# V weights ahead of x tiles 8 and 9 in the load order of a fused attention and gated block

## The chip, the cores and the metric

One core of a Trainium2 chip. The metric is the device time of one launch in microseconds; the granted TensorE clock was 1.000 in every profile, and every timed run counts as in the fast state (single looks are of unknown state by rule). "Look" below means one profiled execution. The span of a profile runs from its first to its last instruction and is some 1.3 us shorter than the device time.

## The reference

x is 2048 tokens of 640. Normalised, it goes through a windowed, dilated attention (32 heads of 20, window 8, dilation 2) with its output weights, and beside it through a gated product block; x and the two results are summed.

```python
xn = _layernorm(A_x)
# A: qkv = xn @ wqkv; each token attends to itself and 7 tokens at distances 2, 4 .. 14; @ wo
# B: (x @ w_gate) * (x @ w_up) @ w_down
return x + A(xn, wqkv, wo) + B(xn, w_gate, w_up, w_down)      # B_x is not used
```

## The kernel before

The kernel is tuned so that TensorE is busy nearly always. SyncE issues the loads of the first part in one list; the order of that list is all that the change touches.

```python
    for half, eng in ((0, "sp"), (1, "act")):     # x tile 0 in two halves
        ...
    x_load(1)
    for c in range(NCH):
        wqkv_load(0, c)          # Q weights, five pieces of 160 KB
    x_load(2)
    x_load(3)
    for c in range(NCH):
        wqkv_load(1, c)          # K weights, five pieces of 160 KB
    for t in range(4, 8):
        x_load(t)                # 160 KB each
    x_load2(8)                   # x tiles 8 and 9, 320 KB
    wqkv_load(2)                 # V weights, 800 KB in one transfer
    x_load2(10)
    x_load(12)
```

TensorE's program in that stretch: the Q weights on tiles 0 and 1 with 128 columns a matmul (source line L492, with the transposes of tile 1, L434, between), K on tiles 0 and 1 (L773, 256 columns), Q and K on the rest of the first 512 tokens (L499, 50 matmuls of 256 columns), then V on the first 512 tokens (L475, 25 matmuls of 512 columns), then Q and K on tokens 512 to 1023 (also L475), and so on.

VectorE normalises a tile ahead of its use. For each tile u its program order is: statistics of u+1, reciprocal of u, aggregate of u+1, apply of u. SyncE then transposes tile u by a DMA into XNT:

```python
    def ln_pace(t):
        while t_ln[0] <= t and n_ln[0] < NT:
            u = n_ln[0]
            ln_stats_a(u + 1)        # L372, waits for the load of x tile u+1
            ln_stats_b(u + 1)        # L378
            ln_rstd(u)
            ln_apply(u, lambda: ln_aggr(u + 1))   # L419, then the DMA transpose of tile u, L423
            ...
```

So the statistics of tile 8 stand ahead of the apply of tile 7, and tile 7 is needed by the projections of tokens 512 to 1023.

## Time and profile before

| | before |
|---|---|
| device time, median of the 3 runs | 252.53 us (252.44 to 253.09) |
| span of the profiled execution | 251.6 us |
| TensorE busy | 247.3 us, 98% |
| last L499 weight load, first V weight load | 18.11, 18.46 us |
| V weights: issued, landed | 9.72, 18.36 us |

How to read it: with TensorE at 98% only a hole in TensorE's work is time. The views that show the one hole near this change are in the prediction. In the chain of waits each line is start, length and what the time went to; in a timeline a bracket gives the idle time of the engine before the instruction and who ended it. PEld is TensorE's loading of weights; SD is the standard deviation of a tile, which ScalarE computes (L385). "The seam" below is where the L499 matmuls end and the V matmuls (L475) begin.

### The profile page before, as it was taken

How to read it: one execution, taken by the hardware profiler on the slowest of the kernel's cores; microseconds unless marked ns; L12 is line 12 of the kernel's file. 1: busy time of each engine (PE TensorE's matmuls, PEld its weight loads, DVE VectorE, ACT ScalarE, POOL GpSimd, SP SyncE). 2: the span in 40 equal slices, each digit the busy share in tenths (PEclk: the TensorE clock that was granted, in tenths of full speed). 3: DMA queues.
4: the chain of work that ended last, by engine and by line, in shares of the span. 5: the costliest groups of instructions: out<-in, count | busy, mean ns of one | idle time of the engine just before them, and what ended most of it. 6: DMA issues, size and time to landing. Idle time of an engine off the chain costs nothing.

```text
span 251.6 us, 3246 instructions
## 1 busy us (share of the span) xinstructions
PE 247.3 (98%) x1274; PEld 129.3 (51%) x1294; DVE 215.8 (86%) x255; ACT 114.6 (46%) x203; POOL 32.6 (13%) x41
## 2 busy tenths in 40 slices
PE   8999999999999999999999999999999999999997
PEld 3995555555544444444444444444444444445775
DVE  5898899999999962999999994899999999996212
ACT  5486667555555557555555552325555111011000
POOL 1000001044434232002231101002000000200200
PEclk9999999999999999999999999999999999999999
DMA  6999779664787563355369972196500011490551
GB/s 187 307 258 206 117 192 409 172 120 82 139 150 127 86 112 55 116 221 98 69 123 257 389 230 42 33 334 63 93 0 3 21 26 36 62 129 21 80 153 52
DMA packets 33775, 33.78 MB, mean 134 GB/s; under 512 B 17984, under 2 KB 30272, under 8 KB 33728
## 3 DMA queue, kind: packets, MB, share of 16 engines
q1 hardware_dynamic: 27280, 24.13, 34.3%
q0 software_dynamic: 6192, 9.31, 22.8%
q8 instruction: 10, 0.16, 0.3%
q10 hardware_dynamic: 288, 0.13, 0.2%
q14 instruction: 5, 0.04, 0.0%
HBM read 14.42 MB, written 4.59 MB: 76 GB/s over the span
## 4 chain that ended last, share of the span: by engine, by line
PE 96%; DVE 1%; ACT 1%; DMA 1%; issue 1%
PE PS L638 41%; PE PS L665 22%; PE PS L475 21%; PE PS L697 7%; PE PS L499 2%; PE PS L773 1%; PE PS L492 1%; DMA XST<-in_A_x_dram 1%; ACT XNS L394 0%; PE PS L434 0%; ACT XNS L392 0%; DVE XNS L419 0%; DVE STATS L372 0%; DVE STATS L378 0%; ACT SD L397 0%
## 5 line engine op out<-in xcount | busy, mean ns | idle before, releaser
L638 PE MATMUL PS<-XNT,WU 128*128 128x512 bf16 x237 | 59.0, 379 | 0.2
L638 PE MATMUL PS<-XNT,WG 128*128 128x512 bf16 x232 | 57.9, 379 | 0.4
L475 PE MATMUL PS<-XNT,WQKV 128*128 128x512 bf16 x245 | 53.7, 379 | 0.4 <-issue 0.2
L605 DVE TENSOR_TENSOR PVB<-VO,ATB 128x10240 f16<-128x10240 bf16 x8 | 43.9, 5488 | 0.2
L475 PEld LDWEIGHTS PS<-XNT,WQKV 128*128 128x128 bf16 x250 | 29.3, 118 | 24.6 <-ACT SD L385 0.2
L640 ACT ACTIVATE USX<-PS 128x512 bf16<-128x512 f32 x48 | 28.7, 597 | 22.6 <-PE PS L638 22.6
L638 PEld LDWEIGHTS PS<-XNT,WU 128*128 128x128 bf16 x240 | 23.5, 98 | 28.3
L638 PEld LDWEIGHTS PS<-XNT,WG 128*128 128x128 bf16 x240 | 23.5, 98 | 28.3
L600 DVE TENSOR_TENSOR PVB<-PVB 128x5120 f16<-128x5120 f16 (+1 forms) x16 | 34.5, 2154 | 0.3
L533 POOL DMA_DIRECT2D LOG<-PE x24 | 21.9, 927 | 58.5 <-DMA LOG<-PE 58.2
L640 ACT ACTIVATE HT<-PS 128x512 bf16<-128x512 f32 x36 | 21.5, 597 | 16.4 <-PE PS L638 16.4
L671 ACT ACTIVATE DT<-PS 128x512 f16<-128x512 f32 x15 | 8.9, 596 | 42.5 <-PE PS L665 39.5
L665 PE MATMUL PS<-HT,WD 128*128 128x512 bf16 x118 | 27.4, 379 | 0.1
L522 DVE TENSOR_TENSOR TMP<-QH,KH 128x2048 f16<-128x2048 bf16 x16 | 19.1, 1217 | 0.3 <-ACT KH L482 0.3
L665 PEld LDWEIGHTS PS<-HT,WD 128*128 128x128 bf16 x120 | 11.7, 98 | 14.2
L522 DVE TENSOR_TENSOR PP<-QH,KH 128x2048 f16<-128x2048 bf16 x16 | 18.9, 1217 | 0.0
L527 DVE TENSOR_TENSOR PP<-PP,TMP 128x4096 f16<-128x4096 f16 x8 | 18.3, 2290 | 0.2
L665 PE MATMUL PS<-VO,WO 128*128 128x512 bf16 x74 | 18.4, 379 | 0.0
L701 DVE TENSOR_TENSOR FOUT<-PS,XR 128x320 bf16<-128x320 f32 (+2 forms) x9 | 4.1, 455 | 15.3 <-PE PS L697 15.3
L533 POOL DMA_DIRECT2D PE<-PP x8 | 8.4, 1044 | 63.4 <-DVE PP L528 63.4
L643 DVE TENSOR_TENSOR HT<-HT,USX 128x512 bf16<-128x512 bf16 x36 | 14.3, 415 | 1.7 <-ACT USX L640 1.7
L482 ACT ACTIVATE VO<-PS 128x512 bf16<-128x512 f32 x20 | 11.9, 595 | 8.2 <-PE PS L475 8.2
(71 smaller groups left out, 222.1 us busy)
## 6 DMA issues: line engine op xcount, KB each, us to landing
PE<-PP POOLq DMA_DIRECT2D x8, 512.0 KB, 4.8
ATB<-LOG SPq DMA_DIRECT2D x8, 512.0 KB, 4.8
LOG<-PE POOLq DMA_DIRECT2D x24, 128.0 KB, 2.7
WG<-in_B_w_gate_dram SPq DMA_DIRECT2D x1, 1920.0 KB, 8.0
WU<-in_B_w_up_dram SPq DMA_DIRECT2D x1, 1920.0 KB, 14.6
WD<-in_B_w_down_dram SPq DMA_DIRECT2D x1, 1920.0 KB, 10.1
out_dram<-in_A_x_dram SPq DMA_DIRECT2D x1, 1920.0 KB, 10.5
out_dram<-FACC POOLq DMA_DIRECT2D x3, 640.0 KB, 6.7
```

Source lines behind the costliest of these rows:

```text
L475: op("pe", (lambda l, x, c: lambda e: e.matmul(PS[:, b, :], l, x, start=(c == 0), stop=(c == NCH - 1)))(l, x, c), r=[l, x], w=[PS[:, b, :] ...
L482: op("act", lambda e: e.activation(o, PS[:, b, :], ACT.Copy, scale=sc), r=[PS[:, b, :]], w=[o], name=f"pev{which}_{m}_{j}")
L522: return (1.22, lambda: op("dve", lambda e: e.tensor_tensor(o, qw, kw, ALU.mult), r=[q, k], w=[o], name=f"prod{h}_{p}_{c}"))
L527: (2.3, lambda: op("dve", lambda e: e.tensor_tensor(a, a, b, ALU.add), r=[a, b], w=[a], name=f"psum{h}_{p}")),
L533: op("pool", lambda e: e.dma_start(o, i, accum_op=ALU.add), r=[o, i], w=[o], dma=True, name=name)
L600: return lambda: op("dve", lambda e: e.tensor_tensor(o, x, y, ALU.add), r=[x, y], w=[o], name=f"{name}_{b}")
L605: lambda: op("dve", lambda e: e.tensor_tensor(PVB[:], vw, aw, ALU.mult), r=[v, a], w=[PVB[:]], name=f"pv_{b}")),
L638: op("pe", (lambda l, x, c: lambda e: e.matmul(PS[:, b, :], l, x, start=(c == 0), stop=(c == NCH - 1)))(l, x, c), r=[l, x], w=[PS[:, b, :] ...
L640: op("act", lambda e: e.activation(o, PS[:, b, :], ACT.Copy), r=[PS[:, b, :]], w=[o], name=f"guev{which}_{m}_{j}")
L643: h_pending.append(lambda: op("dve", lambda e: e.tensor_tensor(h, h, o, ALU.mult), r=[h, o], w=[h], name=f"h{m}_{j}"))
L665: op("pe", (lambda l, x, i: lambda e: e.matmul(PS[:, b, :], l, x, start=(i == 0), stop=(i == n - 1)))(l, x, i), r=[l, x], w=[PS[:, b, :]], ...
L697: op("pe", (lambda l, x, i, b, wid: lambda e: e.matmul(PS[:, b, 0:wid], l, x, start=(i == 0), stop=(i == n - 1)))(l, x, i, b, wid), r=[l, ...
```

## The change

Its intent is to have the V weights in place when TensorE asks for them. Two issues of SyncE change places; no instruction and no byte comes or goes.

```diff
     for t in range(4, 8):
         x_load(t)
+    wqkv_load(2)
     x_load2(8)
-    wqkv_load(2)
     x_load2(10)
     x_load(12)
```

## The prediction

> **What bounds the kernel now.** I read the page first (busy shares, then the chain of work that ended last), then the timeline of each engine around the first use of the V weights, then the transfers issued there one by one, and last the waits of the other engines in the first 32 us. The page:
>
> ```profile
> PE 247.3 (98%) x1274; PEld 129.3 (51%) x1294; DVE 215.8 (86%) x255; ACT 114.6 (46%) x203; POOL 32.6 (13%) x41
> ...
> PE 96%; DVE 1%; ACT 1%; DMA 1%; issue 1%
> ```
>
> TensorE is busy for 98% of the span and is 96% of the chain that ended last. VectorE's 86% is beside it. So a change gains only what idle time of TensorE it removes and loses only what idle time it adds. The chain in order of time, at the place that the diff touches (start, length, what):
>
> ```profile
> 13.03 5.46 PE PS L499 x50
> 18.48 0.23 issue
> 18.71 10.74 PE PS L475 x49
> ```
>
> After 18.71 the chain is unbroken matmul work to 249.79 (the 0.05 us breaks, one after each 49 matmuls, come every 10.79 us and are two matmul steps long: records missing from the trace, not waits). The one hole after 13 us is at 18.48, exactly where the Q and K projections of the first 512 tokens (L499) end and the V projections (L475) begin. The timelines of the weight loads and of SyncE's issues around it:
>
> ```profile
> 18.46 7.50 PEld L475 LDWEIGHTS PS<-XNT,WQKV 128*128 128x128 bf16 x36 [0.24 <-ACT SD L385]
> ```
> ```profile
> 9.72 0.47 SPq L294 DMA_DIRECT2D WQKV<-in_A_wqkv_dram  x1
> ```
>
> and the transfer issues, in windows that hold one new issue each, KB and us to landing:
>
> ```profile
> XST<-in_A_x_dram SPq DMA_DIRECT2D x1, 320.0 KB, 5.8
> ```
> ```profile
> WQKV<-in_A_wqkv_dram SPq DMA_DIRECT2D x1, 800.0 KB, 8.6
> ```
> ```profile
> XNT<-XNS SPq DMA_TRANSPOSE x1, 3.6
> ```
>
> The profile names ScalarE's SD (17.93 to 18.21) as the releaser. I don't believe it: the wait before that weight load is on two semaphores, and V's transfer, issued at 9.72, lands 8.6 us later, by the trace's own increments at 18.36; the waiting instruction ends at 18.44 and the weight load starts at 18.46. It is V's landing. So the intent of the change is to remove this hole by putting V's 800 KB ahead of the 320 KB of x tiles 8 and 9.
>
> How long is it really? The last L499 matmuls start 0.109 us apart, the last at 18.21; the first V matmul starts at 18.71. Without a wait it would start at about 18.21 + 0.11 = 18.32. The hole is **0.39 us**, a little more than the 0.23 that the chain shows, since that counts from a modelled end (a 256-column matmul is shown as 0.27 us).
>
> **What the Trainium skill says.** "TensorE: Matmul & The Clock Gate", section "Wait, 56ns, not 53.3ns?": warm start-to-start is N / 2.4 GHz plus about 2.5 ns. That is 109 ns for 256 columns and 216 ns for 512; the trace has 0.109 and 0.216 us, so what stands between 18.21 and 18.71 beyond one step is waiting. "DMA: Bandwidth & Descriptors", section "Queues, rings and completion order": each DMA engine consumes the descriptors of one row in ring order. The trace agrees: all these loads come from SyncE and land in the order of issue (x7 12.90, x8/9 15.03, V 18.36, x10/11 19.23, x12 19.70). Same page, "Why a DMA increments its semaphore by 16 and not by 1": only the full 16 means landed, so the slowest engine decides. For V the 16 increments run from 15.2; fifteen are there by 17.2 and the last comes at 18.36. The TensorE page, "Architectural detail", says ScalarE and VectorE queues are strict FIFO; this matters below, since they take a late x tile 8 in program order.
>
> **The change, part by part.** No instruction and no byte is added or removed; two issues of SyncE change places, at 9.24 and about 9.7.
>
> V: it is issued 0.48 us earlier and has 320 KB less ahead of it. At the slowest engine the queue moved 800 KB between 15.03 and 18.36, or 240 KB per us (an estimate from these two landings). V, after x7 and with nothing of x8/9 ahead, should land at 18.36 − 320/240 = about **17.0**. TensorE asks at 18.3. A margin of 1.3 us remains, so the hole should go entirely: −0.39 us. Everything behind it on TensorE starts 0.39 earlier.
>
> x tiles 8 and 9: they take V's former place at the end of the same bytes, so they land at about **18.36** instead of 15.03. VectorE starts the statistics of tile 8 at 16.67 now and would idle until about 18.40, **1.7 us**. This matters because in program order those statistics stand ahead of the apply of tile 7: from the start of statistics 8 to the end of apply 7 is 16.67 to 18.10, 1.43 us, so apply 7 ends at 18.40 + 1.43 = 19.83. SyncE is busy with the transpose of tile 6 (17.71, 1.77 us) until 19.48 and issues that of tile 7 at 19.53 now; it would issue it at about 19.88, 0.35 later. That transpose takes 3.6 us to landing, 23.12 now, so about **23.5**. TensorE first needs tile 7 after the 25 V matmuls of the first 512 tokens: 18.32 + 25 × 0.216 = **23.72** (24.11 now). A margin of 0.2 us is left, where it was 1.0. Thin, but no new wait on the estimate.
>
> VectorE afterwards: statistics 9 run at 19.75 and apply 8 at about 21.0 instead of 20.38, where it waits now 1.24 us for the transpose of tile 4 to free a buffer. So 1.1 of the 1.7 us are absorbed there, and a lag of 0.6 remains; it meets a 0.86 us idle before apply 15 at 30.24, again for a buffer, so what gets through is about SyncE's 0.35. The first product at 30.60 would come at about 30.95. TensorE does not read VectorE's work until the output projections: the value products of the first 512 tokens end at 150.37 and the matmuls that read them come 12 steps after 150.32, at 152.9. The slack of 2.5 us covers 0.35 + 0.39.
>
> ScalarE: SD 8 moves from 17.93 to about 19.7 and holds back the K eviction at 18.52 to about 20.0 and the first V eviction from 19.78 to about 20.6. Eight banks rotate; the K eviction's bank (7) is wanted by the second projection of tokens 512 to 1023, at 23.72 + 1.08 = 24.8. No wait. The later loads x10 to x12 have the same bytes ahead of them as before: unchanged. The weights for the gated part are asked for at 72 us and land at 41.5 and 48.7: no matter.
>
> Sum: −0.39 and +0.0 to +0.2 for the thin margin at tile 7: 252.53 − 0.39 + 0.06 = **252.2 us**.
>
> **The rivals.**
> First, the transpose of tile 7 takes the hole's place. For it: the margin of 0.2 us; its own landing is set by one slow engine (fifteen increments by 22.3, the last at 23.1); and x8/9 could land after 18.36. Against: a wait there first eats the gain, and only a landing after 24.11, 1 us later than now, costs anything. It would make 252.3 to 252.6, and with 0.5 us more of delay 253.
>
> Second, V is not early enough, since the slow engine is slow for a reason tied to time and not to bytes (four engines lag from 14 us on, the time when the first transposes are issued). V's fifteen other increments came by 17.2 even behind x8/9, so it would take a straggler over 1.3 us. I give it one in eight; the time stays at 252.5, since then nothing is gained while the late x tiles still hide.
>
> Third, VectorE becomes the bound through 1.7 us of delay. Against: 98% TensorE with the slack shown and idle time for buffers that absorbs it. It would be at most +1.7 us, 254, still within 2%.
>
> **Range and chances.** The three times before span 252.44 to 253.09, 0.65 us, more than the gain. The centre is 252.2; the full gain on a quiet run gives 252.0 to 252.1, no gain on a noisy one 252.8. Range 251.8 to 252.8. Two per cent is 5 us; no single wait that the change touches is a third of that, so faster 0.01, within 2% 0.98, slower 0.01.
>
> **What would show it.** Right: V lands near 17.0; the first V matmul starts 0.11 us after the last L499 one, and the hole is gone from the chain; x8/9 land near 18.4 and VectorE shows a new wait on the x load of about 1.7 us before a statistics instruction; the wait for the tile 4 transpose falls from 1.24 to near 0; the tile 7 transpose is issued near 19.9; and the chain shows no new break near 23.7. Wrong: the hole stands at 18.5 (second rival), a new one at 23.7 to 24.5 with the tile 7 transpose as its releaser (first), or TensorE waits for VectorE near 150 us (third). The count of everything else, 3246 instructions and 33.78 MB, must stay.

## More of the kernel before

V's matmuls are in `proj`:

```python
        for c in range(NCH):
            l, x = wcols(which, c, m), XNT[:, c, j * JB:(j + 1) * JB]
            op("pe", ... e.matmul(PS[:, b, :], l, x, start=(c == 0), stop=(c == NCH - 1)) ...)
```

## The result, and the profile after

| | before | after |
|---|---|---|
| device time, median of 6 runs each | 252.64 us (252.44 to 253.09) | 252.53 us (252.46 to 252.94) |
| ratio | | 0.9997, 95% interval 0.9984 to 1.0009 |
| span of the profiled execution | 251.629 us | 251.630 us |
| V weights landed | 18.36 us | 16.22 us |
| x tiles 8 and 9 landed | 15.03 us | 17.08 us |

A ratio is the mean time of one kernel's runs over the mean of the other's in the same rounds, so it is not quite the ratio of the two medians. The result is "the same": inside the range of the prediction, and with an interval that holds both no gain and a gain of 0.4 us. Every ratio in this document is over the kernel before, also where an experiment's edit is made on the changed kernel.

The first look after, the chain of waits (start, length, what):

```profile
3.08 4.17 DMA WQKV<-in_A_wqkv_dram
7.25 0.14 issue
7.38 0.45 PE PS L492 x5
...
13.21 5.46 PE PS L499 x50
18.67 0.05 issue
18.72 10.74 PE PS L475 x49
```

The hole at the seam is gone: 0.23 us before, 0.05 after. But the span didn't move by a hundredth. The reason stands a few lines higher: the Q and K matmuls began later in this execution. The same place in the chain of the kernel before:

```profile
6.46 0.65 DVE XNS L419 x2
7.11 0.10 issue
7.21 0.45 PE PS L492 x5
```

The matmuls at 7.21 stand at 7.38 after, as TensorE waited for a piece of the Q weights that landed at 7.25 there and at 7.07 before. That piece is issued at 3.08 in both, 6 us ahead of the first issue that the change moves. So in these two looks a late piece took 0.18 us and the mended seam gave 0.17 back. That they cancel to 0.001 us is chance; the experiments show how far these two numbers move from one execution to the next.

The weight loads of TensorE at the seam and V's transfer, after (timeline; transfer issues with KB and us to landing):

```profile
18.39 0.44 PEld L475 LDWEIGHTS PS<-XNT,WQKV 128*128 128x128 bf16 x3
```
```profile
WQKV<-in_A_wqkv_dram SPq DMA_DIRECT2D x1, 800.0 KB, 7.0
```

No bracket, so no idle time before the first V weight load. V took 7.0 us from an issue at 9.25. VectorE, after:

```profile
17.10 0.49 DVE L372 BATCH_NORM_STATS2 STATS<-XST 128x6 f32<-128x320 bf16 x1 [0.21 <-DMA XST<-in_A_x_dram]
```
```profile
20.46 0.45 DVE L419 TENSOR_SCALAR XNS<-XST,MV,SD 128x640 bf16<-128x640 bf16 x1 [0.88 <-DMA XNT<-XNS]
```

The new wait for x tile 8 is there, but 0.21 us long. The wait before the apply of tile 8, for the buffer that the transpose of tile 4 frees, is 0.88 us; it was 1.24.

**How long the hole really was.** The trace has 250 weight loads of L475 and only 245 matmul records. The missing ones are 50 matmuls apart, which makes the breaks of 0.05 us in the chain at 29.45, 40.24 and so on, and one of them is the very first V matmul. A weight load starts when the matmul before it starts (the second V matmul stands at 18.714, the load of the third at 18.715), so the loads show where it was: before, the load of the second V matmul starts at 18.494, after at 18.503. From the last L499 weight load to this one are two steps, 0.218 us, if nothing waits; it was 0.389 before and 0.218 after. The hole was 0.389 − 0.218 = **0.17 us**. The prediction read 0.39 from a record that is the second matmul's. Two later looks (the third and fourth after) have all 250 matmuls and confirm it: there the first V matmul stands at 18.423 and 18.176, within 0.002 us of the second weight load.

### The profile page after: what moved, and what is told of

The parts are those of the page before. It is cut to its first block, busy times and chain, and to the rows that moved or that the text cites. A ratio compares the mean times of both kernels' runs of the same rounds, so it can differ in the third digit from the quotient of the medians.

```text
span 251.6 us, 3246 instructions
## 1 busy us (share of the span) xinstructions
PE 247.3 (98%) x1274; PEld 129.3 (51%) x1294; DVE 215.9 (86%) x255; ACT 114.6 (46%) x203; POOL 32.6 (13%) x41
## 4 chain that ended last, share of the span: by engine, by line
PE 96%; DMA 2%; SPq 1%; issue 1%; DVE 0%
PE PS L638 41%; PE PS L665 22%; PE PS L475 21%; PE PS L697 7%; PE PS L499 2%; DMA WQKV<-in_A_wqkv_dram 2%; PE PS L773 1%; PE PS L492 1%; SPq L294 1%; PE PS L434 0%; DVE FOUT L701 0%
## 5 line engine op out<-in xcount | busy, mean ns | idle before, releaser
L475 PE MATMUL PS<-XNT,WQKV 128*128 128x512 bf16 x245 | 53.7, 379 | 0.3
L475 PEld LDWEIGHTS PS<-XNT,WQKV 128*128 128x128 bf16 x250 | 29.4, 118 | 24.4
L638 PEld LDWEIGHTS PS<-XNT,WU 128*128 128x128 bf16 x240 | 23.5, 98 | 28.3
L638 PEld LDWEIGHTS PS<-XNT,WG 128*128 128x128 bf16 x240 | 23.5, 98 | 28.3
```

What stands on the lines that cost most here:

```text
L475: op("pe", (lambda l, x, c: lambda e: e.matmul(PS[:, b, :], l, x, start=(c == 0), stop=(c == NCH - 1)))(l, x, c), r=[l, x], w=[PS[:, b, :] ...
L638: op("pe", (lambda l, x, c: lambda e: e.matmul(PS[:, b, :], l, x, start=(c == 0), stop=(c == NCH - 1)))(l, x, c), r=[l, x], w=[PS[:, b, :] ...
```

## The experiments

Theory after the first result: TensorE waits at the seam for V's slowest DMA engine and for nothing else; the hole was 0.17 us; the change removes it; VectorE's delay is hidden; and the gain is lost in what the Q and K pieces vary. Rivals: the hole is a fixed cost or ScalarE's SD, as the profile names it; the late x tiles take the gain back; the change itself makes the start late.

All looks together, from the traces (us; "hole" is measured on weight loads as just above; "rest" is the span less the start of the second V weight load):

| look | V order | last L499 load | V landed | hole | span | rest |
|---|---|---|---|---|---|---|
| before | behind x8/9 | 18.11 | 18.36 | 0.17 | 251.63 | 233.135 |
| before, second | behind x8/9 | 18.27 | 17.23 | 0.00 | 251.62 | 233.130 |
| before, third | behind x8/9 | 17.93 | 17.75 | 0.00 | 251.27 | 233.126 |
| before, fourth | behind x8/9 | 17.88 | 17.12 | 0.00 | 251.22 | 233.123 |
| after | ahead | 18.29 | 16.22 | 0.00 | 251.63 | 233.127 |
| after, second | ahead | 17.93 | 15.75 | 0.00 | 251.27 | 233.124 |
| after, third | ahead | 18.21 | 16.15 | 0.00 | 251.55 | 233.126 |
| after, fourth | ahead | 17.96 | 17.20 | 0.00 | 251.30 | 233.123 |
| V read from K (wrong) | behind x8/9 | 17.62 | 18.43 | 0.00 | 251.08 | 233.240 |
| V behind x12 | last | 17.83 | 18.49 | 0.58 | 251.76 | 233.136 |
| x8/9 last | ahead of x10 | 18.41 | 17.56 | 0.00 | 251.75 | 233.124 |
| Q split, first | ahead | 18.33 | 14.92 | 0.00 | 251.67 | 233.124 |
| Q split, second, V behind | behind x8/9 | 17.71 | 16.11 | 0.00 | 251.06 | 233.127 |
| Q split, second, V ahead | ahead | 18.16 | 14.13 | 0.00 | 251.50 | 233.129 |

The last column is the key: from the second V weight load on, an execution takes 233.12 to 233.14 us in 13 of the 14. All that differs between those 13 happens before 18.7 us.

### Both kernels again

No edit in either. Each was timed over 5 rounds (interleaved with the kernel before), then given two further looks on other chips.

> The kernel before, unchanged, timed against itself. My theory (the hole at the start of the V projections was only 0.17 us, since the first V matmul at about 18.49 is missing from the record; the change removes it, and the gain of 0.17 us is smaller than what one execution differs from the next): ratio 1.000 with an interval about 0.001 wide on each side, single runs spread over 0.4 us or more; in the profile the wait before the first V weight load is there again (0.15 to 0.35 us on the weight loads), and the wait near 7 us for a piece of the Q weights has another length than 0.33 us. Rival (the change itself makes the start later by 0.18 us and so gives the gain back): the first matmul on Q pieces after the wait near 7 us stands at 7.20 again, not elsewhere.

> The changed kernel, unchanged, timed again. My theory: no wait before the first V weight load, steps of 0.109 us across the seam, V landing between 16 and 17.5; the place of the matmul after the wait near 7 us differs from 7.38 by 0.1 us or more, in either direction; time 0.9985 to 1.0005 of the kernel before, true ratio 0.9993. Rival (the change makes the start later): the matmul after the wait near 7 us stands at 7.38 again, ratio 1.000.

Measured: the kernel before against itself, median 252.91 (252.61 to 253.44), ratio 1.0011 (0.9998 to 1.0025). The changed kernel, median 252.57 (252.32 to 252.84), ratio 0.9998 (0.9985 to 1.0011). The kernel before of these rounds: median 252.54 (252.37 to 253.02). So a kernel against itself came out further from 1 than the change did. The second look at before held no hole at all. Its weight loads and its chain:

```profile
18.38 0.44 PEld L475 LDWEIGHTS PS<-XNT,WQKV 128*128 128x128 bf16 x3
```
```profile
3.55 4.41 DMA WQKV<-in_A_wqkv_dram
7.96 0.05 issue
8.00 1.87 PE PS L492 x30
...
13.19 5.46 PE PS L499 x50
18.65 0.05 issue
18.70 10.74 PE PS L475 x49
```

V landed at 17.23 in it, in the old order, and another Q piece (7.96) was the late one. The start is not made late by the change: the matmuls after the first Q wait stand at 7.38 in the first look after and at 7.03 in the second.

The looks:

> A third look at the kernel before. My theory (the hole comes and goes with V's slowest engine): V's last engine lands anywhere from 17.0 to 18.5; a hole at the seam only if that is later than TensorE's last 256-column matmul; span = start of the first V weight load + 233.2 us either way. Rival (the hole is a property of the order of loads): hole of 0.17 us again.

> A fourth look at the kernel before, with the same expectations as the third: under my theory two of the four looks at most show the hole, and the spans differ by what the waits for Q and K pieces before 11 us differ, not by the hole alone; under the rival every look but one shows it.

> A third look at the changed kernel, to have as many looks at it as at the kernel before. My theory: V's last engine lands between 15.5 and 17.5, before TensorE asks in any case, so the first V weight load follows the last 256-column one after 0.109 us; x8/9 land between 16 and 18.5, and VectorE's wait for them, if any, ends without a hole on TensorE near 23.5; span = start of the first V weight load + 233.24. Rival (the late x tiles cost as much as V gained): a hole near 23.5.

> A fourth look at the changed kernel, with the same expectations as the third.

Measured: one time each, 252.61 and 252.53 before, 252.85 and 252.64 after; no hole in any of the four. V in the old order landed at 17.12 to 18.36 in four looks while TensorE's last L499 load stood at 17.88 to 18.27: one hole in four. In the new order V landed at 15.75 to 17.20, at least 0.76 us before that last load in each look. The hole of the first look did not come back, and the rival that it belongs to the order as such fell. The spread is not only one of chips: the three looks with this order that were taken on chip 4 (the third and fourth before, and the one without a wait for V further down) have V landing at 17.75, 17.12 and 18.43. In the fourth look after, x8/9 landed at 18.07, near the predicted 18.36, and VectorE waited 1.50 us:

```profile
18.09 0.49 DVE L372 BATCH_NORM_STATS2 STATS<-XST 128x6 f32<-128x320 bf16 x1 [1.50 <-DMA XST<-in_A_x_dram]
```

The wait before the apply of tile 8, for the buffer of tile 4, is gone in this look (1.24 before), as predicted. Its transpose of tile 7 was issued at 19.56 and landed at 22.22; TensorE went on without a hole. So in this look even the late case that the prediction feared is hidden.

### V behind x12: the hole in a larger dose

```diff
         x_load(t)
     x_load2(8)
-    wqkv_load(2)
     x_load2(10)
     x_load(12)
+    wqkv_load(2)
```

(edit on the kernel before; 3 rounds)

> The V weights behind x tiles 10 to 12 instead of ahead of tile 8: 800 KB with all the x tiles ahead of them. My theory (the first V matmul waits for V's landing and for nothing else): V lands near 19.9, the first V matmul starts near 20.0 instead of 18.5, the hole grows from 0.17 to about 1.6 us and the time by the same 1.3 to 1.6 us against the kernel before, 1.0055 of it, as all TensorE work moves along. Rival (the hole is ScalarE's SD, or a fixed cost where 256-column matmuls give way to 512-column ones): the hole stays at 0.2 us and the time is the same.

Measured: 253.14 (253.07 to 253.85), ratio 1.003 (1.0014 to 1.0046), a slowdown clear of 1, though still "the same" by the limit of 2%. Weight loads and V's transfer:

```profile
18.59 0.37 PEld L475 LDWEIGHTS PS<-XNT,WQKV 128*128 128x128 bf16 x3 [0.65 <-ACT SD L385]
```
```profile
WQKV<-in_A_wqkv_dram SPq DMA_DIRECT2D x1, 800.0 KB, 7.7
```

Issued at 10.74, V lands at 18.49 and the first V weight load starts 0.10 us later, as in the first look before (18.36 and 18.46). The hole is V's landing. The profile again names ScalarE's SD, and again wrongly: that SD ended at 18.04. A fixed cost of the change from 256 to 512 columns is ruled out too: twelve of the fourteen looks have none. The size was a miss, 0.58 instead of 1.6 us, since V landed 1.4 us earlier than I had worked out (the last section has what is odd about it). Three of its four times agree within 0.13 us (253.07, 253.08, 253.20), which fits a start that V's landing sets and not the Q pieces; four runs are few to say so.

### V read from the K weights: the most there is to gain

```diff
-            l, x = wcols(which, c, m), XNT[:, c, j * JB:(j + 1) * JB]
+            l, x = wcols(1 if which == 2 and j == 0 else which, c, m), XNT[:, c, j * JB:(j + 1) * JB]
```

(edit on the kernel before; 5 rounds)

> The kernel before, wrong on purpose: the 25 V matmuls of the first 512 tokens read the K weights, which are there long before, so they have no transfer to wait for; every load and every other instruction stays. It measures the most that any earlier V load can gain. My theory now (V's landing behind x8/9 is 17.2 in one look and 18.4 in another, with TensorE asking at 17.9 to 18.4, so the hole is there in some executions only, 0.2 us long): no hole at the seam, ratio 0.999 to 1.000 with an interval that holds 1, so at most 0.2 us. Rival (the hole is in most executions and as long as predicted, 0.39 us, and the changed kernel gives it back elsewhere): ratio 0.9985 or lower, clear of 1.

Measured: wrong (relative error 0.74), 252.45 against 252.65, ratio 0.9995 (0.9983 to 1.0008). With no wait for V at all the gain is still not clear of noise: its best estimate is 0.05%, 0.13 us. A gain of 0.39 us in every execution would be 0.9985, just inside the edge of the interval. The look also shows that the hole can be long in the old order. V landed at 18.43 there, with TensorE's last L499 load at 17.62; with the delays of the first look (a load 0.10 us after the landing, its matmul 0.03 later) the first V matmul would have started at 18.56 instead of 17.84, a hole of some 0.7 us (an estimate). And it shows what is next in line. TensorE, not waiting, was at the projections of tokens 512 to 1023 by 23.1:

```profile
23.32 0.59 PEld L475 LDWEIGHTS PS<-XNT,WQKV 128*128 128x128 bf16 x4 [0.39 <-DMA XNT<-XNS]
```

The transpose of tile 7 landed at 23.27, and this is the first rival of the prediction come true: rest is 233.240 instead of 233.125, so 0.115 us went back. TensorE was early in this look; in none of the four looks after did it wait for this transpose.

### x tiles 8 and 9 last: the late x tile in a larger dose

```diff
     wqkv_load(2)
-    x_load2(8)
     x_load2(10)
     x_load(12)
+    x_load2(8)
```

(edit on the changed kernel; 3 rounds)

> V ahead as in the change, and x tiles 8 and 9 last of all, behind x10 to x12: the late x tile in a double dose. My theory (VectorE's program order puts the statistics of tile 8 ahead of the apply of tile 7, whose transpose TensorE needs at about 23.8): x8/9 land near 19.7, VectorE waits about 3 us before the statistics of tile 8, apply 7 ends near 21.2, the transpose of tile 7 lands near 24.7, and TensorE gets a hole of 0.6 to 1.0 us there; time 0.3 to 0.8 us over the kernel before (1.001 to 1.003). Rival (late x tiles are absorbed whatever their delay, or the transpose queue catches up): no hole after the V projections and the time within 0.1 us of the changed kernel's. Third (VectorE's delay of 3 us reaches the end): time 2 to 3 us longer, 1.01.

Measured: 252.79 (252.43 to 253.25), ratio 1.0008 (0.9993 to 1.0023), not told apart from 1. VectorE and TensorE:

```profile
19.77 0.49 DVE L372 BATCH_NORM_STATS2 STATS<-XST 128x6 f32<-128x320 bf16 x1 [2.43 <-DMA XST<-in_A_x_dram]
```
```profile
23.89 0.26 PEld L475 LDWEIGHTS PS<-XNT,WQKV 128*128 128x128 bf16 x2 [0.17 <-DMA XNT<-XNS]
```

Up to the apply of tile 7 all went as worked out: x8/9 at 19.75, VectorE waiting 2.43 us, apply 7 ending at 20.82 + 0.39 = 21.21, the transpose issued at 21.24. But it landed after 2.6 us, at 23.84, and not after 3.6; the transpose of tile 6 landed at 21.58, so little of SyncE's list was still in flight ahead of it. The load that waited started 0.077 us late, less than the 0.216 us that a load here starts ahead of its matmul (the next load followed after 0.139): rest is 233.124, so nothing was lost. The hole of 0.6 to 1.0 us was a miss. What lengthened this look was a K piece issued at 5.95 and landed at 10.90, which is ahead of everything edited. So 4.7 us more delay of x8/9 than in the kernel before (19.75 against 15.03) cost nothing that shows in this look; the interval of the ratio leaves room for 0.6 us.

### Q pieces by two queues

An attempt to shorten the wait that does vary, and to beat both kernels. First split, edit on the changed kernel (5 rounds):

```diff
     for c in range(NCH):
-        wqkv_load(0, c)
+        wqkv_load(0, c, eng="act" if c % 2 else "sp")
```

> The changed kernel with pieces 1 and 3 of the Q weights issued by ScalarE's queue instead of SyncE's, so that the pieces are asked for earlier. My theory (the time of one execution is set by where the V stage starts, and that by the last engine to land a Q or K piece near 7 us, since after the seam all is constant to 0.01 us): the wait near 7 us falls from 0.3 to 0.6 us to under 0.2 us, the first V weight load starts at 17.7 to 17.9, the span is that plus 233.24, and the time falls by 0.2 to 0.4 us, ratio 0.9985 to 0.9993. Rival (the transfers are bound by the engines that move them, not by their issue): the pieces land as late as now, no gain, ratio 1.000.

Measured: 252.42 (252.30 to 252.96) against 252.65, ratio 0.9993 (0.9981 to 1.0005): not clear of 1. Four of the five runs are at 252.30 to 252.43; the profiled one is the fifth. In it piece 3, issued at 1.89 instead of 3.08, landed at 6.90, where it landed at 6.70 to 7.25 in the eight looks at the two kernels: asked for 1.2 us earlier, it was hardly there earlier. Piece 2, issued at 2.12, landed at 7.07 instead of 5.30 to 5.86. That speaks for the rival in this look. Piece 1 also went ahead of piece 0, which landed at 5.89 instead of 4.24 to 4.94. So a second split kept piece 0 in front, with V in both orders (5 rounds each):

```diff
-        wqkv_load(0, c)
+        wqkv_load(0, c, eng="sp" if c % 2 else "act")
```

> The kernel before (V behind x8/9) with pieces 0, 2 and 4 of the Q weights issued by ScalarE's queue and 1 and 3 by SyncE's, so that piece 0 keeps its place in front. My theory: all later loads are issued about 0.9 us earlier, the waits for Q pieces near 7 us shrink, TensorE asks for V at 17.6 to 17.9, and V behind x8/9 lands at 16.5 to 18.0, so that a hole at the seam stays possible (0 to 0.4 us). Time 0.1 to 0.3 us under the kernel before. Rival (the pieces are bound by the engines that move them): they land as late, time unchanged.

> The same split of the Q pieces with V ahead of x8/9. My theory: V lands near 15, no hole at the seam in any look, the V stage starts as soon as the 256-column matmuls end, span = start of the first V weight load + 233.24; time 0.2 to 0.4 us under the kernel before (ratio 0.998 to 0.9995) and 0 to 0.15 us under the same split with V behind. Rival (order of V matters more once the start is earlier): 0.3 us or more between the two.

Measured: with V behind 252.74 (252.34 to 253.13), ratio 1.0009 (0.9997 to 1.0021); with V ahead 252.90 (252.28 to 254.72), ratio 1.0032 (1.0007 to 1.0057), against 252.49 in these rounds. Both expected a gain, and neither gave one; the one with V ahead is slower, clear of 1. The look with V behind is its fastest run (252.34), so it doesn't show what made the others slower. In the chain of the one with V ahead, the place of the Q piece is taken by x tile 1:

```profile
1.19 3.52 DMA XST<-in_A_x_dram
...
4.74 0.84 ACT XNS L392 x2
5.57 0.02 issue
5.60 0.93 ACT XNS L394 x2
...
7.08 0.36 DVE XNS L419
```

Tile 1 landed at 4.71; it landed at 3.49 to 3.89 in the four looks before. Its normalisation takes 2.7 us to the apply. Whether that also made the runs of 253.73 and 254.72 stays open, since they have no trace here; the latter's granted clock was 0.993, the only one below 1.000. No version that beats both kernels came out of this.

## Why the prediction was right or wrong, point by point

- **The seam hole as V's landing, against the name in the profile: right.** V behind x12 shows it: the load starts 0.10 us after the landing, wherever that is.
- **The length of the hole, 0.39 us: wrong.** This is the term of the sum that was mis-sized. It was 0.17 us in that look, as the matmul taken for the first V one was the second; and it was 0 in the three later looks at the same kernel. The same misreading put the first need for tile 7 "now" at 24.11; from the loads it is 18.494 + 25 × 0.216 = 23.89. The prediction had found the missing records 11 us further on, and did not ask whether one lay at the seam.
- **The hole goes entirely: right**, in four looks of four, though three of the four looks before had none either; what shows it is V's margin of 0.76 us or more. The estimate of V's landing, 17.0, lies in the measured 15.75 to 17.20.
- **x8/9 at 18.36 and 1.7 us of VectorE: right as a mechanism, too large as a rule.** They landed at 16.61 to 18.07 in four looks, and VectorE waited 0.21 us in the first and 1.50 in the fourth. The step that failed is to take the slowest engine's landing of one execution for a property of the bytes ahead. The place in the byte order that V had (after 1,120 KB behind x7) was reached at 18.36, 17.23, 17.75, 17.12 and 18.43 by V, and at 17.08, 16.61, 17.22 and 18.07 by x8/9. The 240 KB per us built on two such landings inherits that spread.
- **The margin at tile 7: right that no hole comes, with a wrong size of its risk.** The issue came at 19.62 for 19.88 and the landing at 23.35 for 23.5 in the first look, but SyncE, busy with tile 6 until 19.57, set the issue there, and not VectorE, whose apply of tile 7 ended at 18.54. In the fourth look it was VectorE (apply ended at 19.53, issue at 19.56), and the landing came after 2.7 us instead of 3.6. The margin was used up in two experiments: without the V wait, where TensorE was early, at a cost of 0.115 us, and with x8/9 last, by 0.077 us at no cost.
- **The rivals.** The tile 7 transpose in place of the hole: not with this change. V not early enough: not seen, the least margin was 0.76 us. VectorE as the bound: no; even 2.43 us of waiting cost nothing that shows.
- **The time: 252.2 predicted, 252.53 measured**, inside 251.8 to 252.8 and in the class given 0.98. The range held because it was drawn around what runs vary, not because the gain was right. With one hole of 0.17 us in four looks the mean gain would be some 0.04 us, a tenth of the predicted one. With the look without a V wait as a fifth, where 0.7 us of waiting were avoided, it would be some 0.18 us, half of it. Both are estimates from few looks, and they differ by one late landing; the run without a V wait gained 0.13 us, not clear of 0. Which size is true stays open: no ratio here resolves it.

## What to carry to other kernels

Before a single hole in a trace is given a length, count the records around it (loads against matmuls) and look a second time: here the hole was less than half as long as it looked and absent in three of four executions. Ask which part of an execution is constant (here everything after 18.7 us, to 0.02 us in 13 of 14 looks) and which varies, since a gain of 0.2 us in the varying part can be seen only in traces. A load order that leaves every consumer a margin wider than the spread of landings (1.3 us here) is safer than one that is on time in one look, even if no timing shows it.

## What the Trainium skill lacked or had wrong

- "DMA: Bandwidth & Descriptors" (sections "Bandwidth" and "Queues, rings and completion order") gives times by size and an order, but no spread from one execution to the next. The same 800 KB behind the same bytes landed between 17.12 and 18.43 us in five looks, and the 160 KB Q piece issued at 3.07 or 3.08 between 6.55 and 7.25 in ten. The page says that only the full count means landed ("Why a DMA increments its semaphore by 16 and not by 1"); how late one engine of 16 can be it does not say (here fifteen increments by 17.24, the last at 18.36, 1.1 us alone).
- The same page says ("Rules for kernel authors") that spreading DMAs over several issuing engines "only saves sequencer issue time". The runs agree that it gains nothing clear (ratios 0.9993, 1.0009, 1.0032). The page says too that the transfers of several issuing engines interleave; what it lacks is by how much one issued first on one queue is slowed by the next on the other. x tile 1 landed at 4.27 and 4.71 in the two looks of the second split and at 3.49 to 4.02 in all others. That suggests a slowing and doesn't show it: the first split also issues a Q piece on ScalarE's queue at 1.41, and tile 1 landed at 3.58 there.
- No page that I read accounts for this: in the nine looks with x12 last and the Q pieces on one queue, the last plain load before the DMA transposes lands on all 16 engines within 0.1 us, some 0.4 us after the slowest engine of the load ahead of it (x12 from 19.61 to 19.70 after 19.23; after 18.10 from 18.47 to 18.55). V behind x12 fits it in part: it landed at 18.41 to 18.49 on all engines, though x12 ahead of it had landed at 16.29. What holds it back is open.
- "Perfetto Trace Analysis" has nothing on matmul records that are missing at a fixed distance; here one of every 50 V, Q and K matmuls of L475 was missing (245 records for 250 loads) in most looks, none in two (250 for 250), and one fell on the instruction in question.
